# A lower scheduling place for the weight-conversion passes while attention runs alone, in a fused attention and feed-forward kernel

## The chip, the core and the metric

The kernel runs on one core of one Trainium2 chip. The metric is the device time of one execution in microseconds (us). Its five engines work side by side and meet through semaphores: TensorE (PE; its weight loads are shown apart as PEld), VectorE (DVE), ScalarE (ACT), GpSimd (POOL) and SyncE (SP), whose queue issues nearly all DMAs. Each engine executes its own list of instructions strictly in the order in which that list was built.

## What is computed

The reference, cut to what matters:

```python
# 8 batches, 8 heads, 512 local and 32 global positions, head size 64, window 32
out_g = softmax(scale * q_g @ concat(k_g, k_l).T) @ concat(v_g, v_l)
s_ll  = where(|i - j| <= 32, scale * q_l @ k_l.T, -1e9)
out_l = softmax(concat(scale * q_l @ k_g.T, s_ll)) @ concat(v_g, v_l)
x = concat(out_g, out_l), laid out as 4608 tokens x 512
h = x @ w_in                          # 512 x 2048
g = where(h > 0, h, exp(min(h, 0)) - 1)
result = g @ w_out                    # 2048 x 512
```

All inputs are float32, save that the host passes the two weight matrices as 64-bit integers that hold float64 values.

## The kernel before

**Attention** (`attention`, line 643 on) runs over 80 slots, one for each batch, head group of four and tile of 128 positions, and one for the global queries of each group. A slot has four stages, and each is one step of the generator: S (scores, line 769, then the masked negative scores and their minimum on VectorE, L780, and the exponentials on ScalarE, L786), T (transposes of the four probability tiles, L809, copied by L811), U (transposes of the global columns, L742 to L745, copied by L746, L748 and L750) and V (products with the values, L853 and L822, into a bank `h`, copied to `xr` by L859 and reduced by L864 to L868). The normalisation by the row sums is L790, L791 and L795 on VectorE and four L793 on GpSimd. The global slots use L703 and L706, L715 and L716, the exponentials L720 and L722, and L731 and L732 on GpSimd. The probability tiles rotate through three buffers, named p_93, p_94 and p_95 in what follows, and the transposed ones through ptw_81 and ptw_82.

**Feed-forward** (`ffn_stream`) takes blocks of 256 tokens as they get ready. `split_x` (L568, L571) splits a block into two float16 parts `xh` and `xl`; `ffn1` (L324) makes `h` from three products per weight tile; L333 to L349 make the activation and its two parts; `ffn2` (L447, and L482 for blocks that use a seven-product scheme) multiplies with `w_out`.

**Conversion** (`load_weights`, `unit`, lines 157 to 226) turns the weights into two float16 parts. A unit is two of sixteen column groups of `w_in` (m = 0) or row groups of `w_out` (m = 1). Its steps are: s0 (L188 on ScalarE takes the magnitude of the upper words, L189 on GpSimd clamps it), s1a (L193), s1b (L196) and s1c (L200), three VectorE passes over 1024 columns that put the bits together, s1d (L204 on ScalarE, which also sums each partition's bound and thereby gives the raw buffer free), s2 (for w_in, L141 and L142, the maximum over the partitions), s3 (L131 to L136 and L213, the high part) and s4 (L216, the low part). Raw weights come by a DMA on SP's queue (L174) into two buffers in turn. Units 0 to 3 (pairs 0 and 1 of w_in and w_out) and unit 4 (pair 2 of w_in) are started while attention runs alone.

**What sets the order.** The main loop takes one step of attention after the other. While `lead[0]` holds (the first 66 steps) the feed-forward only prepares blocks; after that a table of paces says how many feed-forward steps go with each attention step. `defer(n, fn)` runs a function n ticks later. A scheduler then takes all instructions with a priority that follows the order in which the program wrote them, and builds each engine's list from them: at each point the instruction of the best priority that it holds to be ready. `tc.high_priority(offset=-BEHIND)` with BEHIND = 60 puts what is written inside it 60 places back. Before the change only `add_up` (sums of weight blocks, much later) uses it.

Of the kernel before, what the change touches and what calls it, by code (L numbers as in the profile page):

```python
# [44 lines left out]
BEHIND = 60  # L45
# [15 lines left out]
def attn_ffn(ctx: ExitStack, tc: tile.TileContext, qT, qgT, kT, vT, vgT, vpT, w_in, w_out, mask, out):  # L61
# [28 lines left out]
    def tick():  # L90
        now[0] += 1
        for fn in later.pop(now[0], []):
            fn()

    def drain():
        while later:
            tick()

    lead = [True]

# [76 lines left out]
    def unit(m, p, raw):  # L177
        f = slice(2 * p * P, 2 * (p + 1) * P)
        shape = [P, NC, 2 * P] if m == 0 else [P, 2, DM]
        parts = [w[:, :, f] for w in win] if m == 0 else [w[:, 2 * p:2 * p + 2, :] for w in wout]  # L180
        pw = (pww if m == 0 else pwo)[:, p:p + 1]
        u = ffn.tile(shape, F32, name="cu", bufs=3)
        mx = ffn.tile([P, 4], F32, name="cm", bufs=4)
        high, low = raw[..., 1], raw[..., 0]
        ui = u.bitcast(I32)

        def s0():
            nc.scalar.activation(u, high.bitcast(F32), AF.Abs)  # L188
            nc.gpsimd.tensor_scalar(u, u, FMAX, FMIN, ALU.min, ALU.max)  # L189

        def s1a():
            tc.keep_in_program_order(
                nc.vector.tensor_scalar(ui, ui, 3, 0x3ffffff8, ALU.logical_shift_left, ALU.bitwise_and))  # L193

        def s1b():
            nc.vector.scalar_tensor_tensor(out=ui, in0=high, scalar=-0x40000000, in1=ui,  # L196
                                           op0=ALU.bitwise_and, op1=ALU.bitwise_or)

        def s1c():
            nc.vector.scalar_tensor_tensor(out=ui, in0=low, scalar=29, in1=ui,  # L200
                                           op0=ALU.logical_shift_right, op1=ALU.bitwise_or)

        def s1d():
            nc.scalar.activation(low.bitcast(F32), u, AF.Abs, accum_out=mx[:, m:m + 1])  # L204

        def s2():
            if m == 0:
                all_max(mx[:, 1:2], mx[:, 0:1])

        def s3():  # L210
            power(pw, mx[:, 1:2])
            inverse(mx[:, 3:4], pw)
            nc.scalar.activation(parts[0], u, AF.Copy, scale=mx[:, 3:4])  # L213

        def s4():
            nc.vector.scalar_tensor_tensor(out=parts[1].rearrange("p a b -> p (a b)") if m else parts[1],  # L216
                                           in0=u.rearrange("p a b -> p (a b)") if m else u, scalar=mx[:, 3:4],
                                           in1=parts[0].rearrange("p a b -> p (a b)") if m else parts[0],
                                           op0=ALU.mult, op1=ALU.subtract)

        d = 1 if lead[0] else 2
        lag = 7 if m else 16
        for i, fn in ((1, s0), (1 + d, s1a), (1 + 2 * d, s1b), (1 + 3 * d, s1c), (1 + 4 * d, s1d),
                      (1 + lag, s2), (2 + lag, s3), (3 + lag, s4)):
            defer(i, fn)

    def tables(group):

# [30 lines left out]
    def add_up(p, cross):  # L259


        if not sums:
            sums["rows"] = [ffn.tile([P, NP * 512], F16, name="raw") for _ in range(2)]
            sums["diag"] = [ffn.tile([P, NP * 256], F16, name="cu", bufs=3) for _ in range(2)]
        w = ffn.tile([P, 2, DM], F32, name="cu", bufs=3)
        s = ffn.tile([P, 512], F32, name="tmp", bufs=3)
        d = None if cross else ffn.tile([P, 512], F32, name="tmp", bufs=3)[:, 0:256]
        pr = slice(2 * p, 2 * p + 2)
        flat = [a[:, pr, :].rearrange("p a b -> p (a b)")[:, 256:768] for a in wout]
        rows = [a[:, p * 512:(p + 1) * 512] for a in sums["rows"]]  # L270
        diag = [a[:, p * 256:(p + 1) * 256] for a in sums["diag"]]
        todo = ((flat, s),) if cross else ((rows, s), (diag, d))

        def s0():
            nc.vector.tensor_add(w, wout[0][:, pr, :], wout[1][:, pr, :])

        def s1():
            if cross:
                nc.vector.tensor_sub(s, w[:, 1, :], w[:, 0, :])
            else:  # L280
                nc.vector.tensor_add(s.rearrange("p (a b) -> p a b", a=2), w[:, :, 0:256], w[:, :, 256:512])
                nc.vector.tensor_add(d, w[:, 0, 0:256], w[:, 1, 256:512])

        def s2():
            for dst, src in todo:
                nc.scalar.copy(dst[0], src)

        def s3():
            for dst, src in todo:
                nc.vector.tensor_sub(dst[1], src, dst[0])  # L290
            if cross:
                added.append(p)

        def behind(fn):
            with tc.high_priority(offset=-BEHIND):
                fn()

        for i, fn in enumerate((s0, s1, s2, s3)):
            defer(1 + 2 * i, lambda fn=fn: behind(fn))
# [774 lines left out]
```

## Time and profile before

| | us |
|---|---|
| median of three runs | 953.43 |
| lowest and highest run | 948.69, 953.65 |
| the profiled execution | 954.72 |
| its span from first to last instruction | 952.9 |

The profiled execution lies 1.29 us above the median, and 1.8 us of it lie around the span. In the span PE is busy for 908.5 us, VectorE for 728.1, ScalarE for 670.1 and GpSimd for 271.1. A busy PE is not a PE at its peak, since matmuls are pipelined. The first matmul of the feed-forward starts 77 us into the span. Names in the rows read out<-in; what stands in brackets at a row's end is the time that the engine sat idle before it and what ended that.

### The profile page before, as it was taken

The page shows a single profiled execution, that of the slowest core. Times are in us where ns is not written, and L with a number is a line of the kernel's source. Part 1 is how long each engine was busy: PE and PEld are TensorE (multiplying, and loading weights), DVE is VectorE, ACT ScalarE, POOL GpSimd, SP SyncE. Part 2 cuts the span into 40 slices and gives each one's busy share as a digit, 9 for nine tenths or more (in the row PEclk, how much of TensorE's full clock was granted, in tenths as well). Part 3 has the DMA queues.
Part 4 walks back from the last instruction along what each step waited for, and adds up shares of the span by engine and source line. Part 5 has one row for each costly group of instructions (what it writes and reads, how often), then busy time and mean ns, then how long its engine had stood idle before and what let it go on. Part 6 is the DMA issues. An engine that isn't in the chain of part 4 may idle for free.

```text
span 952.9 us, 23830 instructions
## 1 busy us (share of the span) xinstructions
PE 908.5 (95%) x9216; PEld 727.8 (76%) x9216; DVE 728.1 (76%) x2025; ACT 670.1 (70%) x1584; POOL 271.1 (28%) x483
## 2 busy tenths in 40 slices
PE   6889887899999999999999999999999999999997
PEld 3567564566666788888888888888888888888886
DVE  4988988889967777768776877687777777676566
ACT  5888996776656767757677767677767767666564
POOL 4655481461522322122121212221332312100000
PEclk8779999899999999999999999999999999999999
DMA  6855876331342023101330123102310101000000
GB/s 262 299 179 180 282 224 191 124 123 57 115 157 90 23 100 103 47 26 46 105 121 26 46 78 125 47 27 79 122 49 25 46 23 35 2 23 23 1 24 23
DMA packets 41769, 87.64 MB, mean 92 GB/s; under 512 B 7736, under 2 KB 8888, under 8 KB 41656
## 3 DMA queue, kind: packets, MB, share of 16 engines
q1 hardware_dynamic: 41368, 85.85, 26.6%
q8 instruction: 73, 1.20, 0.5%
q14 instruction: 40, 0.33, 0.1%
q10 hardware_dynamic: 288, 0.26, 0.1%
HBM read 70.89 MB, written 15.20 MB: 90 GB/s over the span
## 4 chain that ended last, share of the span: by engine, by line
PE 67%; DVE 14%; ACT 9%; POOL 3%; issue 3%; DMA 3%; SPq 0%; DVEq 0%; ACTq 0%; POOLq 0%
PE pa L324 25%; PE acc L482 12%; PE h L482 9%; PE acc L447 4%; PE pa L822 3%; PE h L324 3%; PE pa L769 3%; PE pa L809 2%; ACT p L786 2%; DMA raw<-w_out 2%; PE pa L889 2%; DVE gl L345 1%; POOL p L793 1%; DVE cu L196 1%; DVE cu L200 1%
## 5 line engine op out<-in xcount | busy, mean ns | idle before, releaser
L324 PEld LDWEIGHTS <-winh 128*128 128x128 f16 x2160 | 209.4, 98 | 39.2 <-issue 8.4
L793 POOL TENSOR_SCALAR p<-p,sm 128x128 f32<-128x128 f32 x256 | 147.8, 593 | 303.2 <-DVE sm L791 165.0
L324 PE MATMUL pa<-xh,winh 128*128 128x256 f16 x824 | 224.9, 273 | 0.1
L324 PE MATMUL pa<-xl,winh 128*128 128x256 f16 x824 | 224.6, 273 | 0.0
L324 PE MATMUL pa<-xh,winl 128*128 128x256 f16 x824 | 224.6, 273 | 0.0
L361 ACT ACTIVATE gh<-gx,xs 128x896 f16<-128x896 f32 x103 | 107.3, 1042 | 123.1 <-DVE gx L358 123.0
L345 DVE SCALAR_TENSOR_TENSOR gl<-gx,xs,gh 128x896 f16<-128x896 f32 x103 | 119.4, 1159 | 59.9 <-ACT gh L361 59.0
L482 PEld LDWEIGHTS <-gh 128*128 128x128 f16 x1456 | 139.5, 98 | 24.0 <-issue 7.4
L786 ACT ACTIVATE p<-p,m 128x160 f32<-128x160 f32 x256 | 106.7, 421 | 41.6 <-DVE m L780 41.4
L324 PEld LDWEIGHTS <-winl 128*128 128x128 f16 x1080 | 106.1, 98 | 14.3 <-issue 1.2
L333 ACT ACTIVATE g<-pa,xs 128x512 f32<-128x512 f32 x103 | 70.3, 682 | 24.4 <-PE pa L324 23.8
L482 PE MATMUL acc<-wouth,gh 128*128 128x256 f16 x312 | 85.2, 273 | 0.0
L482 PE MATMUL acc<-woutl,gh 128*128 128x256 f16 x312 | 85.1, 273 | 0.0
L335 ACT ACTIVATE g<-g 128x512 f32<-128x512 f32 x135 | 85.0, 630 | 0.1
L482 PE MATMUL acc<-wouth,gl 128*128 128x256 f16 x312 | 85.0, 273 | 0.0
L482 PEld LDWEIGHTS <-gl 128*128 128x128 f16 x728 | 71.2, 98 | 9.2 <-DVE gl L345 1.0
L482 PE MATMUL h<-raw,gh 128*128 128x256 f16 x416 | 75.0, 273 | 0.0
L324 PE MATMUL h<-xh,winh 128*128 128x256 f16 x256 | 71.1, 279 | 1.5 <-ACT hs L334 0.9
L324 PE MATMUL h<-xl,winh 128*128 128x256 f16 x256 | 71.0, 278 | 0.7 <-DVE xl L571 0.7
L324 PE MATMUL h<-xh,winl 128*128 128x256 f16 x256 | 71.0, 278 | 0.0
L780 DVE CUSTOM_DVE_ANT_0 p<-pa,msk 128x160 f32<-128x160 f32 x228 | 61.5, 318 | 4.8 <-PE pa L769 4.7
L342 DVE SCALAR_TENSOR_TENSOR gx<-g,hs 128x512 f32<-128x512 f32 x51 | 35.9, 704 | 36.0 <-ACT g L335 35.6
(236 smaller groups left out, 2016.9 us busy)
## 6 DMA issues: line engine op xcount, KB each, us to landing
k<-kT SPq DMA_DIRECT2D x32, 640.0 KB, 5.1
v<-vT SPq DMA_DIRECT2D x64, 256.0 KB, 2.8
q<-qT SPq DMA_DIRECT2D x32, 256.0 KB, 5.6
raw<-w_in SPq DMA_DIRECT2D x8, 1024.0 KB, 5.9
raw<-w_out SPq DMA_DIRECT2D x8, 1024.0 KB, 6.8
out<-o SPq DMA_DIRECT2D x32, 256.0 KB, 2.3
od<-o SPq DMA_DIRECT2D x24, 256.0 KB, 3.1
o<-od SPq DMA_DIRECT2D x24, 256.0 KB, 2.8
```

Source lines behind the costliest of these rows:

```text
L324: nc.tensor.matmul(h[:, j, :], wt[:, c, f], xt[:, c, :], start=k == 0, stop=k == 11)
L333: nc.scalar.activation(g, hf, AF.Relu, scale=sc[:, p:p + 1])
L335: nc.scalar.activation(g, g, AF.Exp, scale=-1.0)
L342: nc.vector.scalar_tensor_tensor(out=out, in0=ins[0], scalar=-1.0, in1=ins[1], op0=ALU.add, op1=ALU.max)
L345: nc.vector.scalar_tensor_tensor(out=dst, in0=src, scalar=sg, in1=hi, op0=ALU.mult, op1=ALU.subtract)
L361: nc.scalar.activation(gh, gx, AF.Copy, scale=sg)
L447: nc.tensor.matmul(acc[t], gt[:, s], wt[:, f, :], start=p == first and j == 0 and k == 0, stop=p == last and j == 1 and k == 2)
L482: nc.tensor.matmul(cols, gt, w, start=p == 0 and k == 0, stop=last and k == len(todo) - 1, skip_group_check=True)
L769: nc.tensor.matmul(sp[r][half * HQ:(half + 1) * HQ, j * KW:(j + 1) * KW], q[rows, qs], k[rows, t, half, :], start=True, stop=True)
L780: nc.vector.tensor_tensor_reduce(out=p, in0=sp[r][:, j * KW:(j + 1) * KW], in1=msk[:, mi, :], op0=ALU.add, op1=ALU.min, scale=-scale, scal ...
L786: nc.scalar.activation(ps[i], ps[i], AF.Exp, bias=m[:, i:i + 1], scale=-1.0, accum_out=s[:, 0, i:i + 1])
L793: nc.gpsimd.tensor_scalar(ps[i][:, 0:P], ps[i][:, 0:P], s[:, 1, i:i + 1], 1.0, ALU.mult, ALU.mult)
```

## The change

A helper `behind` moves from `add_up` to the head of the kernel, and the deferred steps of a conversion unit are wrapped in it if the unit is started while attention runs alone. Steps s0 and s2 keep their place; s1a to s1d, s3 and s4 get a place 60 back. What is computed stays the same, instruction by instruction.

```diff
+    def behind(fn):
+        with tc.high_priority(offset=-BEHIND):
+            fn()
+
     lead = [True]
...
         lag = 7 if m else 16
         for i, fn in ((1, s0), (1 + d, s1a), (1 + 2 * d, s1b), (1 + 3 * d, s1c), (1 + 4 * d, s1d),
                       (1 + lag, s2), (2 + lag, s3), (3 + lag, s4)):
-            defer(i, fn)
+            defer(i, (lambda fn=fn: behind(fn)) if lead[0] and fn not in (s0, s2) else fn)
...
             if cross:
                 added.append(p)
-
-        def behind(fn):
-            with tc.high_priority(offset=-BEHIND):
-                fn()
 
         for i, fn in enumerate((s0, s1, s2, s3)):
             defer(1 + 2 * i, lambda fn=fn: behind(fn))
```

In the changed kernel the lines of `unit` stand four lower: L188 is L192 there, L193 is L197, L196 is L200, L200 is L204, L204 is L208 and L142 is L146.

The lists of all engines differ in about the first 125 us and are the same, apart from those line numbers, from there to the end. Three places:

VectorE, before, about 43 us into the span, where the three passes of unit 3 stand; the names p_93, p_94 and p_95 are probability tiles of three successive slots:

```order
L795 TENSOR_TENSOR pz<-p_93,sm 128x128
L193 TENSOR_SCALAR cu<-cu 128x1024
L811 COPY ptw_81<-pa 128x2x4x64
L196 SCALAR_TENSOR_TENSOR cu<-raw,cu 128x1024
L142 TENSOR_REDUCE cm<-pa 128x1
L200 SCALAR_TENSOR_TENSOR cu<-raw,cu 128x1024
L753 TENSOR_REDUCE ptg_84<-pa 128x32
L131 TENSOR_SCALAR pww<-cm 128x1
L790 TENSOR_SCALAR sm<-sm 128x4
L780 ISA p_95,m<-pa,msk 128x160
```

VectorE, after, the same passes of unit 3:

```order
L753 TENSOR_REDUCE ptg_84<-pa 128x32
L791 RECIPROCAL sm<-sm 128x4
L780 ISA p_95,m<-pa,msk 128x160
L780 ISA m 128x1
L795 TENSOR_TENSOR pz<-p_94,sm 128x128
L197 TENSOR_SCALAR cu<-cu 128x1024
L811 COPY ptw_82<-pa 128x2x4x64
L200 SCALAR_TENSOR_TENSOR cu<-raw,cu 128x1024
L864 COPY xglob<-h 128x2x32
L868 TENSOR_REDUCE xm<-xr 128x1
L204 SCALAR_TENSOR_TENSOR cu<-raw,cu 128x1024
```

The three passes have moved from behind the slot of p_93 to behind that of p_94, past the four L780 of p_95, and the last of them stands behind the copy L864, which needs a product of PE.

ScalarE, before, about 62 us into the span, around the magnitude pass L188 of unit 5 (the second pair-2 unit, not itself wrapped):

```order
L786 ACTIVATE p_94,sm<-p_94,m 128x160 x2
L188 ACTIVATE cu<-raw 128x1024
L568 ACTIVATE xh<-xr,xm 128x1024
L720 ACTIVATE pg,sg<-pa,mg 128x4x64 x2
L722 ACTIVATE pu,sg<-pa,mg 128x32
L746 COPY ptw_81<-pa 64x4x32
L748 COPY ptw_81<-pa 64x4x32
L750 COPY ptg_84<-pa 128x2x64
L786 ACTIVATE p_95,sm<-p_95,m 128x160
```

ScalarE, after, the same place:

```order
L568 ACTIVATE xh<-xr,xm 128x1024
L786 ACTIVATE p_94,sm<-p_94,m 128x160 x2
L746 COPY ptw_81<-pa 64x4x32
L748 COPY ptw_81<-pa 64x4x32
L750 COPY ptg_84<-pa 128x2x64
L786 ACTIVATE p_95,sm<-p_95,m 128x160
L192 ACTIVATE cu<-raw 128x1024
L720 ACTIVATE pg,sg<-pa,mg 128x4x64 x2
L722 ACTIVATE pu,sg<-pa,mg 128x32
```

The magnitude pass, which waits for a DMA, has moved back by the first L568, three copies and one exponential; the L720 still follow it.

PE, before, at the same time (`wm` and `xm` transposes are L141; ptw_81 and ptw_82 hold transposed tiles of two slots):

```order
L141 MATMUL pa<-ident,xm 128x128
L809 MATMUL pa<-ident,p_94 128x128 x4
L742 MATMUL pa<-ident,pz 128x128
L745 MATMUL pa<-ident,pg 128x128
L769 MATMUL pa<-k,q 64x160 x3
L853 MATMUL h<-ptg_84,ptw_83 64x160 x2
L822 MATMUL h<-ptw_81,v 64x96 x4
L853 MATMUL h<-ptg_84,ptw_83 64x160 x2
L822 MATMUL h<-ptw_81,v 64x96 x4
L769 MATMUL pa<-k,q 64x160 x5
```

PE, after:

```order
L145 MATMUL pa<-ident,xm 128x128
L853 MATMUL h<-ptg_84,ptw_83 64x160 x2
L822 MATMUL h<-ptw_81,v 64x96 x4
L853 MATMUL h<-ptg_84,ptw_83 64x160 x2
L822 MATMUL h<-ptw_81,v 64x96 x4
L809 MATMUL pa<-ident,p_94 128x128 x4
L742 MATMUL pa<-ident,pz 128x128
L745 MATMUL pa<-ident,pg 128x128
L769 MATMUL pa<-k,q 64x160 x8
```

The value products of one slot have moved ahead of the transposes of p_94, and the eight score products stand together behind those.

## Rows read from the trace of the kernel before

**Rows 1.** The page's granted TensorE clock in 40 slices, tenths of 2.4 GHz.

```profile
PEclk8779999899999999999999999999999999999999
```

**Rows 2.** Busy time by stage: length, then PE, PEld, DVE, ACT, POOL, clock, DMA.

```profile
20.00:78.00 58.00, 48.70 (x533) 34.77 (x534) 50.29 (x214) 44.56 (x148) 36.33 (x76) 0.78 0.61 206
78.00:125.00 47.00, 43.62 (x434) 30.66 (x432) 42.10 (x120) 44.73 (x113) 24.24 (x38) 1.00 0.74 253
125.00:260.00 135.00, 120.59 (x951) 79.61 (x949) 121.35 (x269) 99.28 (x207) 59.08 (x77) 0.96 0.41 134
260.00:953.00 693.00, 682.31 (x7199) 576.10 (x7197) 506.65 (x1388) 471.31 (x1083) 142.91 (x271) 1.00 0.17 57
```

**Rows 3.** The same view, of three short stretches of the lead.

```profile
40.00:52.00 12.00, 11.50 (x77) 7.71 (x75) 10.82 (x45) 8.70 (x30) 8.59 (x14) 0.50 0.87 314
...
66.00:68.00 2.00, 0.18 (x1) 0.21 (x2) 1.21 (x1) 2.00 (x8) 1.78 (x4) 0.61 0.04 13
...
70.00:72.00 2.00, 2.00 (x18) 1.48 (x17) 1.56 (x8) 1.49 (x7) 1.72 (x5) 0.50 0.01 4
```

**Rows 4.** Groups by line, first 78 us: busy us, mean ns, idle before.

```profile
L786 ACT ACTIVATE p<-p,m 128x160 f32<-128x160 f32 x49 | 20.5, 423 | 2.5 <-DVE m L780 2.4
...
L200 DVE SCALAR_TENSOR_TENSOR cu<-raw,cu 128x1024 int32<-128x1024 int32 x4 | 5.0, 1239 | 0.0
L196 DVE SCALAR_TENSOR_TENSOR cu<-raw,cu 128x1024 int32<-128x1024 int32 x4 | 4.9, 1217 | 0.0
...
L216 DVE SCALAR_TENSOR_TENSOR winl<-cu,cm,winh 128x1024 f16<-128x1024 f32 x2 | 2.6, 1282 | 0.0
```

**Rows 5.** Timeline of POOL, 41 to 50 us: start, length, instruction, idle before.

```profile
41.02 1.51 POOL L793 TENSOR_SCALAR p<-p,sm 128x128 f32<-128x128 f32 x4 [0.54 <-ACT p L786]
43.51 4.14 POOL L793 TENSOR_SCALAR p<-p,sm 128x128 f32<-128x128 f32 x4 [0.97 <-DVE sm L791]
...
48.86 1.41 POOL L793 TENSOR_SCALAR p<-p,sm 128x128 f32<-128x128 f32 x4
```

**Rows 6.** Timeline of DVE, 44 to 52 us.

```profile
44.86 1.22 DVE L196 SCALAR_TENSOR_TENSOR cu<-raw,cu 128x1024 int32<-128x1024 int32 x1
...
46.20 1.21 DVE L200 SCALAR_TENSOR_TENSOR cu<-raw,cu 128x1024 int32<-128x1024 int32 x1
...
51.90 0.23 DVE L864 COPY xglob<-h 128x64 f32<-128x64 f32 x1 [0.46 <-ACT xr L859]
```

**Rows 7.** Timeline of ACT, 64 to 74 us.

```profile
64.60 1.13 ACT L188 ACTIVATE cu<-raw 128x1024 f32<-128x1024 f32 x1 [1.61 <-DMA raw<-w_out]
65.63 1.13 ACT L568 ACTIVATE xh<-xr,xm 128x1024 f16<-128x1024 f32 x1
66.67 0.46 ACT L720 ACTIVATE pg<-pa,mg 128x256 f32<-128x256 f32 x1
...
73.17 0.37 ACT L859 COPY xr<-h 128x256 f32<-128x256 f32 x1 [1.69 <-PE h L822]
```

**Rows 8.** Timeline of PE, 67 to 78 us.

```profile
67.82 1.08 PE L809 MATMUL pa<-ident,p 128*128 128x128 f32 x4 [2.41 <-ACT pg L720]
...
70.51 0.80 PE L853 MATMUL h<-ptg,ptw 128*64 128x160 f32 x4
...
73.06 0.85 PE L769 MATMUL pa<-k,q 64*64 64x160 f32 x10
...
77.15 0.27 PE L324 MATMUL h<-xh,winh 128*128 128x256 f16 x1
```

**Rows 9.** Timeline of DVE, 66 to 75 us.

```profile
66.79 2.14 DVE L571 SCALAR_TENSOR_TENSOR xl<-xr,xm,xh 128x1024 f16<-128x1024 f32 x1 [1.52 <-ACT xh L568]
...
73.58 0.23 DVE L864 COPY xglob<-h 128x64 f32<-128x64 f32 x1 [1.51 <-ACT xr L859]
...
74.25 0.31 DVE L780 CUSTOM_DVE_ANT_0 p<-pa,msk 128x160 f32<-128x160 f32 x1
```

**Rows 10.** Timeline of SP's queue, 56 to 59 us.

```profile
56.99 0.38 SPq L174 DMA_DIRECT2D raw<-w_out  x1
58.74 0.33 SPq L681 DMA_DIRECT2D v<-vT  x1
```

## The prediction, made before the result was known

> **What bounds the kernel now.** I read the stages first [rows 2]. From 260 us to the end PE is busy 682.31 of 693 us at full clock: nothing that the change touches lies there, and the engines' lists are the same from about 125 us on, so whatever is won or lost before that point is carried to the end as a shift. The stage that the change rearranges is the lead, 20 to 78 us. There no engine is full: VectorE 50.29 of 58 us, PE 48.70, ScalarE 44.56, GpSimd 36.33. So VectorE has 7.7 us of idle time in it, and that is about the most that a better order can take out of the lead. PE's 48.70 are inflated, since the granted clock is 0.78 on average: the page's clock line is below 9 in slices 1, 2, 3 and 4 [rows 1], and the short stretches show why that matters [rows 3]. Between 40 and 52 us and again around 70 us the clock is 0.50, the lower level of 1.2 GHz, and PE is busy nearly all the time; the second of these comes straight after 66 to 68 us, in which PE ran for 0.18 of 2 us. So the lead is a chain that hops between engines, each waiting for another in turn, with PE at half rate after its longest gap. The two waits to look at are the one before that gap, and the one on GpSimd around 44 us.
>
> **The change part by part.** It adds and removes no work. It moves s1a to s1d, s3 and s4 of units 0 to 4 back, past instructions of attention. A pass costs 1.22 to 1.28 us [rows 4], and each that stood before an instruction of attention lets that one go earlier by as much, if nothing else holds it, and is itself due later.
>
> First place, 40 to 57 us. Before, the passes of unit 3 run at 44.86 and 46.20 us [rows 6] while GpSimd normalises p_93, which takes it 4.14 us; the slots on either side take 1.51 and 1.41 [rows 5]. After, they stand behind p_94's slot, and the four L793 of p_93 lie beside the small L780 instead: 4.14 - 1.51 = 2.6 us off that step. The Trainium skill's GPSIMD Engine Reference (Specifications) says that GpSimd's SBUF interface is shared with VectorE and contended by instructions with two SBUF inputs or in a two-port mode; these rows agree. By that rule the loss moves to p_94, beside which the passes now stand. Worked from the rows alone: p_94's step, started at about 46 us and stretched to 4.14, would end at about 50.1 us, against 50.3 before (48.86 + 1.41), so nobody sees it. Of the 2.6 us PE can use only a part, because it is itself busy 11.5 of 12 us at the half clock there [rows 3]; I take 1.2 us at the copy L859 around 51 us. That is given back: before, the last pass and one L216 were done by the time VectorE came to L864, which waited 0.46 us for L859 [rows 6]. After, L204 and both L216 stand behind L864, and VectorE reaches L864 early and waits there for some 2 us with nothing before it. I take half of the 1.2 us as left at 57 us, 0.6, while one L216 of 1.28 us is still due that was done before. The term lies between a gain of 0.6 us (the L216 finds a hole) and a loss of 0.7 (it doesn't: 1.28 - 0.6); I take 0, the middle.
>
> Second place, 62 to 74 us, where most of the sum comes from. Before, ScalarE stands idle for 1.61 us in front of L188, which waits for raw w_out; then come L188 (1.03 us to the next start), L568 (1.04), and only at 66.67 us the L720 that free a bank for PE's L809 of p_94. PE waits 2.41 us for that, to 67.82 us [rows 7, 8]. After, L568, three copies (some 0.27 us each, estimated at two thirds of an exponential's 0.42 [rows 4]) and one exponential go first: 1.04 + 0.8 + 0.42 = 2.26 us, which fills the 1.61. ScalarE was free at 64.60 - 1.61 = 62.99 us, so L720 starts at 62.99 + 2.26 + 1.03 = 66.3 us, 0.4 earlier, and L809 at 67.4. The larger part is on PE. The value products L853 and L822, which before ran from 70.51 to 73.06 us, stand after the change in front of L809. They need the copy L811 on VectorE, which stands behind L571 there: 64.0 + 1.28 for L571, then some 1.0 us to L753, so they start at about 66.4 us. Two bounds follow, by PE's clock. At the half clock they take 2.55 us, to 68.9; L809 to the first three scores take 70.51 - 67.82 = 2.69, to 71.6; the other five scores (73.06 to 73.84, 0.78 us at what was then a rising clock), to 72.4: 1.45 us before 73.84. At the full clock the first two are halved: 66.4 + 1.27 + 1.35 + 0.4 = 69.4, so 4.4 us before. I take the middle, 2.9 us, because the hole on PE is shortened from both sides but not closed. What was late next before was L859 at 73.17 us, 1.69 us idle in front of it for PE's L822, and L864 on VectorE after 1.51 us idle [rows 7, 9]; both come before L780 of the next slot at 74.25 us. With the products ahead these waits go, and the second L571 is next, at about 71 us: 3 us earlier, so it does not cut the term. L324 then starts at about 74.2 instead of 77.15 us [rows 8].
>
> DMAs. Unit 3's s1d gives the raw buffer free for the DMA at 56.99 us [rows 10]; it is moved back behind L864, to about 51.9 + 0.5 + 1.24 + 1.13 = 54.8 us (L864 and the reduction behind it, the pass, and a ScalarE pass as long as L188). That is 2.2 us before SP's queue comes to it, so it costs nothing; if it ends later than 57 us, the queue stops with the value loads of 58.74 us behind it. From 78 to 125 us ScalarE is busy 44.73 of 47 us and VectorE 42.10 [rows 2]; unit 4's passes move by one or two places among them, which I set at nothing, with up to 0.5 us either way, a third of one pass.
>
> The sum: 0 - 2.9 + 0 = -2.9 us against the profiled execution's 954.72 us, which gives 951.8. It lay 1.29 us above the median of the runs; against the median of 953.43 the same sum gives 950.5 us.
>
> **The rivals.** Half a per cent, 4.8 us, is about what a measurement of this kernel can tell from no change.
>
> *Given back.* VectorE and ScalarE have the same work as before, and ScalarE has 2.3 us of idle time between 78 and 125 us. If PE's earlier start at L324 only makes it wait for L333 and L342, the 2.9 us are lost there. For it speaks ScalarE's 44.73 of 47 [rows 2]; against it, that the waits removed at 63 and 73 us are waits of ScalarE and VectorE themselves. Time: 953.4 us.
>
> *The clock stays up.* If PE never goes idle for long, both stretches at 0.50 shrink. The second gives its upper bound of 4.4 us. In the first, PE's 11.5 busy us would be halved, but only the part between p_93's last L793 at 47.65 us and the copy before L864 at 51.90 is on the path, some 4 us, which gives 2. Time: 953.43 - 6.4 = 947.0 us. For it speaks that L853 and L822 now fill the gap; against, that they can start only at 66.4 us.
>
> *SP's queue stops, slower.* The price is above: if unit 3's s1d ends after 57 us, each us later delays the value loads, and with them stage V and PE. PE falls to 1.2 GHz after such a gap, as at 68 us, and 12 us at half rate, as from 40 to 52, cost 6. It decides at 2.2 us more delay than I count. Time: 953.43 + 6 = 959.4 us. For it speaks that L204, L208 and two copies stand in a row behind L864; against, the 2.2 us.
>
> That the change doesn't do what it says is out: the lists show the passes moved.
>
> **How the numbers follow.** The forecast, 950.5 us, 0.47: a gain of 1.45 to 4.4 us with 0.5 either way, 948.5 to 952.5. Given back 0.20, clock up 0.22, queue stops 0.11. The range reaches from 945.5 (1.5 us below the clock case, for the scatter of the three runs) to 956.0 (2.5 above the given-back case, likewise); it leaves out the queue case and the far end of the clock case. Faster by over 0.5% (below 948.7): the clock case and the lowest tenth of the forecast, 0.28. Slower (above 958.2): the queue case, 0.11. Within: 0.61.
>
> **What would show it.** In the profile after: L793 of p_93 near 1.5 us and of p_94 near 4; no DMA wait of over 0.5 us in front of the magnitude pass at 65 us; L853 ahead of L809 with the granted clock above 0.61 in the two us after; L324 first at about 74 us; the end shifted by the same amount. The forecast is wrong if L324 starts at 74 us and the stage to 125 us gives it back, if L324 starts no earlier than 76.5, or if the raw w_out DMA is issued later than 57 us.

## The result

The changed kernel takes 955.72 us (median of 15 runs, 951.78 to 960.72) against 951.29 us for the kernel before (15 runs, 947.94 to 954.94). The ratio is 1.0046 with a 95% interval from 1.0027 to 1.0064: slower by 4.4 us, between 2.6 and 6.1. The forecast was faster by 2.9 us. A second set of runs, after_again below, gave 955.8 us and the same ratio. One run of after_scales_late (5056.73 us), one of scalar_steps_only (1529.8) and one of the kernel before (1528.71) lie far above all others and are left out of every median and ratio here.

The profiled execution of the changed kernel took 955.26 us, 0.5 below its median, and the one of before took 954.72, which is 3.4 above the 951.29 of its fifteen runs. So the two spans, 953.3 and 952.9 us, are nearly equal though the kernels are not: a comparison of the two traces to the end would hide the loss. It has to be read by stages, and from more than one execution. One instruction serves as a mark, on VectorE the L345 behind the fourth L455, just past the place up to which the lists differ. Here it is in before and in the changed kernel:

```profile
132.57 0.75 DVE L345 SCALAR_TENSOR_TENSOR gl<-g,xs,gh 128x512 f16<-128x512 f32 x1 [0.39 <-ACT gh L349]
```

```profile
136.18 0.75 DVE L345 SCALAR_TENSOR_TENSOR gl<-g,xs,gh 128x512 f16<-128x512 f32 x1 [0.39 <-ACT gh L349]
```

The changed kernel is 3.6 us late there. Its second execution comes to the mark at 136.32 us, two more with before's lead (before_again, pair2_only) at 133.93 and 131.95. So the loss is made ahead of 133 us. What follows hides it: from there to 260 us before_again gains 4.1 us on before, though both execute the same lists.

The windows of the changed kernel, by stage, to be set beside [rows 2] (length, then busy us of PE, PEld, DVE, ACT and POOL with counts, granted clock, DMA share, GB/s):

```profile
20.00:78.00 58.00, 42.28 (x523) 31.38 (x524) 50.22 (x215) 45.26 (x153) 38.50 (x77) 0.85 0.60 206
78.00:125.00 47.00, 43.55 (x410) 29.56 (x409) 37.71 (x109) 39.40 (x94) 19.43 (x36) 0.93 0.67 231
125.00:260.00 135.00, 122.33 (x982) 82.01 (x981) 124.29 (x278) 103.00 (x219) 61.16 (x78) 0.97 0.43 141
260.00:953.00 693.00, 682.78 (x7201) 575.96 (x7199) 507.54 (x1390) 471.73 (x1083) 140.14 (x271) 1.00 0.17 57
```

The last stage is as before (682.78 busy us of PE, 682.31 in [rows 2]). In the lead PE's clock is better, 0.85 against 0.78, and PE is busy for 42.28 us instead of 48.70; that much of the hoped-for effect is there, though part of it is chance (a second execution of before has a clock of 0.82). But from 78 to 125 us the clock is 0.93 where it was 1.00, and the row counts 410 instructions of PE there instead of 434 (424 in before_again): the changed kernel enters that stage late.

**First place, 40 to 57 us.** GpSimd, the L793 of p_93 and p_94:

```profile
44.19 1.46 POOL L793 TENSOR_SCALAR p<-p,sm 128x128 f32<-128x128 f32 x4 [2.16 <-DVE cm L146]
46.89 3.06 POOL L793 TENSOR_SCALAR p<-p,sm 128x128 f32<-128x128 f32 x4 [1.24 <-PE pa L809]
```

The L793 of p_93 now take 1.46 us instead of 4.14, and those of p_94 take 3.06 instead of 1.41 [rows 5], as the prediction had it. What it had not is a little later, on ScalarE's timeline and then PE's:

```profile
53.72 0.26 ACT L746 COPY ptw<-pa 64x128 f32<-64x128 f32 x1 [0.48 <-PE pa L745]
53.88 1.13 ACT L208 ACTIVATE raw<-cu 128x1024 f32<-128x1024 f32 x1
55.10 0.26 ACT L748 COPY ptw<-pa 64x128 f32<-64x128 f32 x1
55.39 0.27 ACT L750 COPY ptg<-pa 128x128 f32<-128x128 f32 x1
...
58.77 1.15 ACT L217 ACTIVATE wouth<-cu,cm 128x1024 f16<-128x1024 f32 x1
```

```profile
55.70 0.44 PE L853 MATMUL h<-ptg,ptw 128*64 128x128 f32 x4 [1.65 <-ACT ptg L750]
...
62.34 0.79 PE L769 MATMUL pa<-k,q 64*64 64x160 f32 x16 [1.66 <-ACT ptg L750]
```

Unit 3's s1d (L208) stands between two copies of one slot, L746 and L748. In before the same step ran at 47.44 us, and s3 of `w_out` (L213 there, L217 here, 58.77 us) ran at 53.76, each ahead of where the copies came due. Now PE waits 1.65 and 1.66 us for L750.

**Second place, 62 to 74 us.** ScalarE and then PE, to be set beside [rows 7, 8]:

```profile
67.84 1.11 ACT L192 ACTIVATE cu<-raw 128x1024 f32<-128x1024 f32 x1
68.86 0.45 ACT L720 ACTIVATE pg<-pa,mg 128x256 f32<-128x256 f32 x1
```

```profile
68.94 0.49 PE L853 MATMUL h<-ptg,ptw 128*64 128x160 f32 x4 [0.20 <-DVE ptg L753]
...
70.29 0.65 PE L809 MATMUL pa<-ident,p 128*128 128x128 f32 x4
...
73.42 0.44 PE L853 MATMUL h<-ptg,ptw 128*64 128x128 f32 x4 [1.03 <-ACT ptg L750]
```

The magnitude pass (L192) no longer waits for its DMA, L853 goes ahead of L809, and the granted clock is 1.00 from 66 to 72 us where it was 0.61 and 0.50 [rows 3]. L853 of the next slot starts at 73.42 us; in before it was 73.84:

```profile
73.84 0.44 PE L853 MATMUL h<-ptg,ptw 128*64 128x128 f32 x4
```

So everything that this place gave has only paid for what was lost between 53 and 63 us.

**Third place, 70 to 82 us, which the prediction did not name.** GpSimd, then PE:

```profile
69.57 1.04 POOL L193 TENSOR_SCALAR cu<-cu 128x1024 f32<-128x1024 f32 x1
70.69 0.26 POOL L584 TENSOR_SCALAR xs<-isc,xm 128x1 f32<-128x1 f32 x1
...
71.85 0.26 POOL L588 TENSOR_SCALAR xs<-wm_b,xm 128x1 f32<-128x1 f32 x1
72.08 2.42 POOL L731 TENSOR_SCALAR pk<-pu,sg 32x32 f32<-32x32 f32 x4
74.59 0.69 POOL L732 TENSOR_SCALAR pg<-pg,sg 128x512 f32<-128x512 f32 x1
...
76.05 2.13 POOL L793 TENSOR_SCALAR p<-p,sm 128x128 f32<-128x128 f32 x6
```

```profile
76.48 1.54 PE L809 MATMUL pa<-ident,p 128*128 128x128 f32 x4 [1.31 <-POOL p L793]
...
78.45 0.42 PE L324 MATMUL h<-xh,winh 128*128 128x256 f16 x1
...
82.31 0.77 PE L769 MATMUL pa<-k,q 64*64 64x160 f32 x16
```

In before GpSimd did L731 and L732, and only then the small scales of the second block, L584 to L588:

```profile
69.69 1.36 POOL L731 TENSOR_SCALAR pk<-pu,sg 32x32 f32<-32x32 f32 x4 [1.83 <-ACT ptw L746]
...
71.81 0.27 POOL L584 TENSOR_SCALAR xs<-isc,xm 128x1 f32<-128x1 f32 x1
...
74.01 2.59 POOL L793 TENSOR_SCALAR p<-p,sm 128x128 f32<-128x128 f32 x4
```

Here six of the scales go first, most likely because both chains became ready at once (the last VectorE steps before them, L728 and L140, start at 70.53 and 70.61 us; in before they, L728 and L136, were at 69.38 and 71.00). L731 starts at 72.08, beside the VectorE pass L571 (72.03 us, 1.32), and takes 2.42 us. The L793 of p_95 start at 76.05 us instead of 74.01. PE waits 1.31 us for them, its clock falls (0.74 from 75 to 80 us), and the first of the L324 run at half rate (0.42 us each instead of 0.27): the first 24 last from 78.45 to 82.31 us, 3.86 us where before took 2.71 (77.15 to the L769 at 79.86).

### The profile page after: what moved, and what is told of

It reads as the page before. It is cut to its first block, busy times and chain, and to the rows that moved or that the text cites. A ratio compares the mean times of both kernels' runs of the same rounds, so it can differ in the third digit from the quotient of the medians.

```text
span 953.3 us, 23839 instructions
## 1 busy us (share of the span) xinstructions
PE 904.5 (95%) x9216; PEld 725.6 (76%) x9216; DVE 727.3 (76%) x2025; ACT 669.6 (70%) x1584; POOL 267.8 (28%) x483
## 4 chain that ended last, share of the span: by engine, by line
PE 68%; DVE 15%; ACT 9%; issue 3%; POOL 2%; DMA 2%; SPq 0%; DVEq 0%; ACTq 0%; POOLq 0%
PE pa L324 25%; PE acc L482 12%; PE h L482 9%; PE acc L447 4%; PE h L324 4%; PE pa L822 4%; PE pa L769 3%; PE pa L809 2%; ACT p L786 2%; PE pa L889 2%; DVE gl L345 1%; DVE cu L200 1%; DVE cu L204 1%; DVE g L342 1%; PE pa L703 1%
## 5 line engine op out<-in xcount | busy, mean ns | idle before, releaser
L324 PEld LDWEIGHTS <-winh 128*128 128x128 f16 x2160 | 209.4, 98 | 39.8 <-issue 8.8
L793 POOL TENSOR_SCALAR p<-p,sm 128x128 f32<-128x128 f32 x256 | 141.1, 567 | 310.2 <-DVE sm L791 169.5
L324 PE MATMUL pa<-xh,winh 128*128 128x256 f16 x824 | 224.9, 273 | 0.1
L324 PE MATMUL pa<-xl,winh 128*128 128x256 f16 x824 | 224.6, 273 | 0.0
L324 PE MATMUL pa<-xh,winl 128*128 128x256 f16 x824 | 224.6, 273 | 0.0
L345 DVE SCALAR_TENSOR_TENSOR gl<-gx,xs,gh 128x896 f16<-128x896 f32 x103 | 119.6, 1161 | 59.9 <-ACT gh L361 59.0
L324 PEld LDWEIGHTS <-winl 128*128 128x128 f16 x1080 | 106.1, 98 | 14.2 <-issue 1.0
L324 PE MATMUL h<-xh,winh 128*128 128x256 f16 x256 | 71.2, 280 | 2.0 <-ACT hs L334 1.4
L324 PE MATMUL h<-xl,winh 128*128 128x256 f16 x256 | 71.1, 279 | 0.7 <-DVE xl L571 0.7
L324 PE MATMUL h<-xh,winl 128*128 128x256 f16 x256 | 71.0, 278 | 0.0
L780 DVE CUSTOM_DVE_ANT_0 p<-pa,msk 128x160 f32<-128x160 f32 x228 | 61.3, 318 | 8.0 <-PE pa L769 7.9
```

The costliest lines, as they stand in the source:

```text
L324: nc.tensor.matmul(h[:, j, :], wt[:, c, f], xt[:, c, :], start=k == 0, stop=k == 11)
L345: nc.vector.scalar_tensor_tensor(out=dst, in0=src, scalar=sg, in1=hi, op0=ALU.mult, op1=ALU.subtract)
L780: nc.vector.tensor_tensor_reduce(out=p, in0=sp[r][:, j * KW:(j + 1) * KW], in1=msk[:, mi, :], op0=ALU.add, op1=ALU.min, scale=-scale, scal ...
L793: nc.gpsimd.tensor_scalar(ps[i][:, 0:P], ps[i][:, 0:P], s[:, 1, i:i + 1], 1.0, ALU.mult, ALU.mult)
```

## Experiments

Theories after the result. **A**: the loss is made at 53 to 63 us by the late ScalarE steps. **B**: it is made after 80 us by unit 4. **C**: it is made at 70 to 82 us by GpSimd's order and PE's clock behind it. **D**: chance arrivals of raw weights decide, not the order. All ratios are to the kernel before.

### One pair alone

The two kernels differ from the changed one in one line:

```diff
-            defer(i, (lambda fn=fn: behind(fn)) if lead[0] and fn not in (s0, s2) else fn)
+            defer(i, (lambda fn=fn: behind(fn)) if lead[0] and p == 1 and fn not in (s0, s2) else fn)
```

and `p == 2` for the other.

> Only units 2 and 3 (pair 1) have their steps put back; pairs 0 and 2 stay as before the change. Theory A (units 2 and 3 lose about 3.0 us at 53 to 63 us, because their late ScalarE steps s1d and s3 run ahead of attention's copies, win 3.4 at 63 to 74 and lose 2.4 at 74 to 82, where GpSimd is late and the clock falls): about 1 to 2.5 us above the kernel before, ratio 1.001 to 1.0026, and the first L324 at 77 to 79 us. Theory B (the loss is made after 90 us, by unit 4): the same as before within 1 us, ratio 0.999 to 1.001. Theory D (only chance waits for raw weights differ): ratio 1.000, and no steady shift behind 82 us.

> Only unit 4 (pair 2 of w_in) has its steps put back; everything up to about 80 us is as before the change. Theory A: ratio 0.999 to 1.001, since unit 4's passes were set at nothing within 0.5 us. Theory B: the whole 4.4 us, ratio 1.0046, with the shift made between 85 and 130 us.

Measured: pair 1 alone 954.32 us, ratio 1.003 (1.001 to 1.0051); pair 2 alone 950.52 us, ratio 1.0004 (0.9982 to 1.0027). B's full loss (1.0046) lies outside the interval of pair 2 alone, and its L345 mark lies at 131.95 us against 135.00 with pair 1 alone: units 2 and 3 carry most of the loss, so B is not the main cause. PE in pair1_only:

```profile
71.75 0.44 PE L853 MATMUL h<-ptg,ptw 128*64 128x128 f32 x4 [1.04 <-ACT ptg L750]
...
74.79 1.02 PE L809 MATMUL pa<-ident,p 128*128 128x128 f32 x3 [1.30 <-POOL p L793]
76.38 0.48 PE L809 MATMUL pa<-ident,p 128*128 128x128 f32 x1 [0.57 <-POOL p L793]
...
77.29 0.42 PE L324 MATMUL h<-xh,winh 128*128 128x256 f16 x1
...
81.07 0.77 PE L769 MATMUL pa<-k,q 64*64 64x160 f32 x16
```

L853 comes at 71.75 us, 2.1 us earlier than in before. Then the L809 wait for GpSimd's L793 twice, 1.30 and 0.57 us, and the first 24 L324 take 3.78 us. This kernel is ahead at 72 us and behind at 81: not what A says, and what C says.

In pair2_only the lists are those of before up to about 77 us, so it is also another execution of that lead. ScalarE there:

```profile
62.54 1.14 ACT L192 ACTIVATE cu<-raw 128x1024 f32<-128x1024 f32 x1
```

No wait for raw `w_out`, where [rows 7] has 1.61 us. The largest wait that the forecast wanted to fill is not there in every execution.

### ScalarE's steps alone, VectorE's passes alone

```diff
-            ... if lead[0] and fn not in (s0, s2) else fn)
+            ... if lead[0] and fn in (s1d, s3) else fn)
```

and `(s1a, s1b, s1c, s4)` for the other.

> Only the ScalarE steps (s1d, and s3 with its small VectorE operations) are put back; the VectorE passes s1a, s1b, s1c and s4 keep the place of before. Theory A in its narrow form (ScalarE's s1d and s3 come late because VectorE's passes in front of them come late): with the passes in place nothing is lost at 53 to 63 us, ratio 0.998 to 1.001. Rival (the place of the ScalarE steps itself is what costs): 3 to 4.4 us, ratio 1.003 to 1.0046.

> Only the VectorE passes (s1a, s1b, s1c, s4) are put back; s1d and s3 keep the place of before. Theory A in its narrow form: the ScalarE steps wait for the late passes all the same and then run ahead of the copies with full preference, so the loss at 53 to 63 us stays: 3 to 5 us above before, ratio 1.003 to 1.005. Rival (the place of the ScalarE steps itself is what costs): ratio 0.997 to 1.001.

Measured: ScalarE's steps alone 955.12 us, ratio 1.0032 (1.0012 to 1.0052); VectorE's passes alone 953.02 us, ratio 1.0016 (0.9997 to 1.0035). The narrow form of A falls: with the passes in place the ScalarE steps cost as much, and the passes alone cost less than was expected. By their numbers the rival fares better: 1.0032 lies in its range (1.003 to 1.0046), 1.0016 just above its other one (0.997 to 1.001), with an interval that reaches into both theories' ranges. But the traces show another wait than the rival names. In both PE waits for GpSimd again, for the L793 of p_94 in scalar_steps_only, which stand behind the eight scales of the first block there (first row of PE's timeline below; ScalarE had also waited 2.00 us for raw `w_out` at 63.36 us), and for those of p_95 in vector_passes_only (second):

```profile
69.49 1.52 PE L809 MATMUL pa<-ident,p 128*128 128x128 f32 x4 [2.69 <-POOL p L793]
```

```profile
72.60 1.42 PE L809 MATMUL pa<-ident,p 128*128 128x128 f32 x4 [1.61 <-POOL p L793]
...
74.45 0.42 PE L324 MATMUL h<-xh,winh 128*128 128x256 f16 x1
...
78.52 0.78 PE L769 MATMUL pa<-k,q 64*64 64x160 f32 x16
```

VectorE's passes alone bring the first L324 to 74.45 us, 2.7 us before the kernel before, but the 24 matmuls take 4.07 us, the first 13 of them at about half rate, so that half of it is lost by 78.5 us.

### Before once more

> The kernel before, profiled a second time. Theory D (the 1.61 us that ScalarE waited for raw w_out at 64.60 us, and the 3.09 us at 158.9 us, are chance arrivals of two DMAs in one execution): in this profile at least one of the two waits is below 0.5 us, the first L324 comes at 75.9 to 77.2 us, and the time is 949 to 951 us where the wait at 159 us is missing and 953 to 955 us where it is there. Rival (both waits belong to the kernel): 1.6 and 3 us again, first L324 at 77.1 us.

Measured: 952.15 us, one run. ScalarE waited 1.90 us for raw `w_out`:

```profile
64.08 1.12 ACT L188 ACTIVATE cu<-raw 128x1024 f32<-128x1024 f32 x1 [1.90 <-DMA raw<-w_out]
```

and 1.01 us at 157.64 us, where the first execution waited 3.09; the first L324 came at 77.01 us. The expectation asked for one wait below 0.5 us, so as written it was missed. With pair2_only there are three executions of this lead: the wait was 1.61, 1.90 and 0 us, the first L324 came at 77.15, 77.01 and 75.92. A fourth execution with the same lists up to 70 us (before_scales_late) waited 1.48 us, so three of four had a wait of 1.5 to 1.9. D is right in that a microsecond in the lead, and up to three at 159 us, are chance; it does not explain a ratio that two sets of runs gave alike.

### GpSimd's scales behind the L793

The eight scales of the second block are queued on GpSimd behind the four L793 of p_95. No other engine's list changes. This is not the order of before, where all eight stand ahead of these L793.

```diff
-                        return group, blk, xh, xl, scales(group, mx), seven
+                        return group, blk, xh, xl, late(scales, group, mx), seven
...
-                    nc.gpsimd.tensor_scalar(ps[i][:, 0:P], ps[i][:, 0:P], s[:, 1, i:i + 1], 1.0, ALU.mult, ALU.mult)
+                    norms.append(nc.gpsimd.tensor_scalar(ps[i][:, 0:P], ps[i][:, 0:P], s[:, 1, i:i + 1], 1.0, ALU.mult, ALU.mult))
...
+    def late(fn, *a):
+        calls.append(1)
+        if len(calls) not in (3, 4):
+            return fn(*a)
+        with tc.issue_after(norms[43].ins):
+            return fn(*a)
```

> The changed kernel, with the eight small GpSimd operations of the second block's scales (L584 to L588, 2.2 us together) held behind the four L793 of p_95; the lists of the other engines stay as they are. Theory C (the late L793 of p_95 and the fall of the clock behind it cost 2.4 us at 74 to 82 us): L793 of p_95 starts at 73 to 74 us instead of 76.05, the first L324 comes at 75.5 to 77 us instead of 78.45, and the time falls by 2 to 3.5 us against the changed kernel's 955.7, ratio to before 1.001 to 1.0025. Rival (PE and VectorE set that place, GpSimd's lateness is covered): no change, ratio 1.0046.

Measured: 952.22 us, ratio 1.0026 (1.0003 to 1.0049). That is 3.5 us below the changed kernel's median and 1.9 us by the ratios, whose intervals overlap. GpSimd's timeline, PE's, and the window from 75 to 80 us:

```profile
70.46 1.36 POOL L731 TENSOR_SCALAR pk<-pu,sg 32x32 f32<-32x32 f32 x4 [0.79 <-DVE xm L140]
71.91 1.56 POOL L732 TENSOR_SCALAR pg<-pg,sg 128x512 f32<-128x512 f32 x1
73.90 1.18 POOL L793 TENSOR_SCALAR p<-p,sm 128x128 f32<-128x128 f32 x3 [0.43 <-DVE sm L791]
```

```profile
73.02 0.44 PE L853 MATMUL h<-ptg,ptw 128*64 128x128 f32 x4 [1.91 <-ACT ptg L750]
...
74.69 1.12 PE L809 MATMUL pa<-ident,p 128*128 128x128 f32 x4
...
75.97 0.27 PE L324 MATMUL h<-xh,winh 128*128 128x256 f16 x1
...
78.69 0.77 PE L769 MATMUL pa<-k,q 64*64 64x160 f32 x16
```

```profile
75.00:80.00 5.00, 4.97 (x53) 3.91 (x52) 4.87 (x21) 4.36 (x19) 4.66 (x12) 1.00 0.16 52
```

The L853 starts at 73.02 us, within 0.1 us of after_again's 73.05. From there on there is no wait for L793, the clock is 1.00 from 75 to 80 us, the first L324 comes at 75.97, and the 24 take 2.72 us. At this place C is shown: it was worth 2 us before the L324 and 1.1 in them. The gain is still there at the L345 mark, 132.04 us against 136.18 and 136.32, which is level with the kernel before (132.57 and 133.93).

### s1d held behind the copies

Unit 3's s1d is queued on ScalarE behind the L750 of the slot whose copies it split (`copies` collects the L750, number 6 is that one). No other engine's list changes.

```diff
-            nc.scalar.activation(low.bitcast(F32), u, AF.Abs, accum_out=mx[:, m:m + 1])
+            hold(nc.scalar.activation(low.bitcast(F32), u, AF.Abs, accum_out=mx[:, m:m + 1]), 6 if (m, p) == (1, 1) else None)
```

> The changed kernel, with one ScalarE instruction moved by two places: s1d of unit 3 (L208 at 53.88 us) is held behind the copies L748 and L750 that it ran ahead of; the lists of the other engines stay as they are. Theory A (PE's 1.65 us wait for L750 at 55.70 us is a loss on the path): PE's L853 starts at 54.5 to 54.8 instead of 55.70 us and everything behind it comes about 1 us earlier, 954.4 to 955.0 us, ratio to before 1.0033 to 1.004. Rival (the wait only takes the place of another one at 56 to 63 us): no change within 0.3 us, ratio 1.0046.

Measured: 954.29 us, ratio 1.0044 (1.0029 to 1.006). PE:

```profile
54.55 0.44 PE L853 MATMUL h<-ptg,ptw 128*64 128x128 f32 x4 [0.54 <-ACT ptg L750]
...
56.47 0.55 PE L822 MATMUL h<-ptw,v 128*64 128x96 f32 x8 [0.47 <-DVE pwo L136]
...
58.29 0.32 PE L145 MATMUL pa<-ident,wm_b 128*128 128x128 f32 x1 [0.73 <-DVE sg L727]
...
61.97 0.79 PE L769 MATMUL pa<-k,q 64*64 64x160 f32 x16 [1.66 <-ACT ptg L750]
```

L853 starts at 54.55 us, 1.15 earlier, as expected. It buys nothing: PE now waits 0.47 and 0.73 us for VectorE behind it, and the L769 of 61.97 us still waits 1.66 for L750, 0.37 us earlier than in the changed kernel and no earlier than in after_again (61.94). The rival holds: taking away this one wait only uncovers the next, since s3 and four exponentials still stand ahead of the second group of copies.

### VectorE's passes of pairs 0 and 1, with the scales held

```diff
-            ... if lead[0] and fn not in (s0, s2) else fn)
+            ... if lead[0] and p < 2 and fn in (s1a, s1b, s1c, s4) else fn)
```

together with the hold of the scales.

> Only the VectorE passes (s1a, s1b, s1c, s4) of pairs 0 and 1 are put back, and the second block's scales on GpSimd are held behind the L793 of p_95. If theories A and C are right, this keeps the earlier start of the value products and leaves out the late ScalarE steps, the late L793 and pair 2: first L324 at 73 to 75 us, 948.5 to 950.5 us, ratio to before 0.997 to 0.9995. Rival (the lead has other limits, and what is won up to 80 us is given back by 125 us): ratio 1.000 to 1.002.

Measured: 950.19 us, ratio 1.0005 (0.9984 to 1.0026). The first L324 came at 75.94 us, later than the 73 to 75 expected: in this execution PE's clock was 0.81 from 65 to 70 us and 0.85 from 70 to 75, where vector_passes_only had 1.00 in the first of these. It was also the slowest of the twelve runs (956.82 us). Not faster than before; the rival's ratio stands for this one.

### The changed kernel again, and two more holds

> The changed kernel, timed and profiled a second time beside the two kernels below. Theory C: L793 of p_95 starts at 75 to 77 us again, PE waits about 1 us for it, the granted clock falls at 76 to 82 us and the first 24 L324 take 3.5 to 4 us instead of 2.5; ratio to before 1.003 to 1.0055. Rival (the late L793 was chance in one execution): the first 24 L324 in 2.5 us, started before 77.5 us.

Measured: 955.8 us, ratio 1.0046 (1.0027 to 1.0064). The L793 of p_95 at 75.66 us, 1.30 us of wait on PE, the first L324 at 78.07 and the 24 in 3.88 us. The third place is no chance of one execution.

> The change for pairs 0 and 1 alone (VectorE and ScalarE steps of units 0 to 3), unit 4 as before, and the second block's scales on GpSimd held behind the L793 of p_95. If GpSimd's lateness is all that the change costs in the lead and unit 4 costs nothing: first L324 at 75.5 to 77 us, 949.5 to 952.5 us, ratio 0.999 to 1.002. Rival (what is left of the loss, 1 to 2.5 us, is made before 70 us by the late passes of pair 1): ratio 1.002 to 1.0035.

The edit is `p < 2` in the line of `defer`, with the hold. Measured: 951.06 us, ratio 0.9996 (0.9978 to 1.0013): nothing is left of the loss. Against after_scales_late only unit 4 differs. That would be 2.8 us for unit 4, but the two intervals overlap, and pair2_only, with unit 4 alone, lost nothing. At the L345 mark this kernel is at 133.10 us, no earlier than after_scales_late's 132.04, so the traces show no such cost up to there. What unit 4's passes cost in company of the others stays open.

> The kernel before, with the second block's scales on GpSimd held behind the L793 of p_95; its lists change in other places too, since the planner answers to the hold. In before GpSimd is hardly late there (PE waits 0.15 us for L793 in the execution without the wait for raw w_out), so theory C expects little: first L324 0 to 0.7 us earlier, ratio 0.9985 to 1.0005. If GpSimd's 2.2 us of scales were on the path in before too: ratio 0.997 to 0.9985, and this kernel would be the fastest of all.

Measured: 949.09 us, ratio 0.999 (0.9965 to 1.0015). In the trace only GpSimd's list differs from before's, at 71 to 76 us; the expectation that other places change too did not come true. The first L324 came at 74.55 us, 2.6 before the kernel before and more than the 0.7 expected. It was given back at once:

```profile
78.00:125.00 47.00, 44.25 (x398) 30.67 (x395) 40.29 (x116) 40.52 (x101) 19.80 (x36) 0.89 0.73 244
```

The row counts 398 instructions of PE between 78 and 125 us, where before has 434 [rows 2], and the clock was 0.89 instead of 1.00; the L345 mark is at 133.13 us, 0.6 behind before. An earlier start of the feed-forward is not yet an earlier end.

> The run of pair 1 alone (ratio 1.003, first L324 at 77.29 us after waits of 1.30 and 0.57 us for L793), now with the second block's scales held behind the L793 of p_95. Theory C: neither wait for L793, first L324 about 3 us behind the L853 before it as in the other two kernels with the hold, so at 74.5 to 75.5 us, and 2 to 3.5 us less than pair 1 alone: ratio 0.9985 to 1.001. If the gain in the lead reached the end in full, it would be the fastest kernel, ratio 0.997 to 0.998. Rival (in pair 1's kernel the loss is made elsewhere): ratio 1.002 to 1.004.

Measured: 949.68 us, ratio 0.9993 (0.9971 to 1.0014), from 1.003 without the hold. The first L324 came at 76.27 us, not at 74.5 to 75.5, since PE waited 2.06 us for L750 ahead of its L853; the part behind it is as expected, 2.96 us. The L345 mark moves from 135.00 us without the hold to 131.65.

All the lead's executions in one table; L853 and the first L324 are starts on PE's timeline, L853 being the first one of the slot ahead of the L809 of p_95, "24 L324" is the time from the first L324 to the L769 behind the first 24, and L345 is the start of the mark on VectorE:

| kernel | L853 | first L324 | between | 24 L324 | L345 | ratio |
|---|---|---|---|---|---|---|
| before | 73.84 | 77.15 | 3.31 | 2.71 | 132.57 | |
| before_again | 73.53 | 77.01 | 3.48 | 2.71 | 133.93 | |
| pair2_only (same lead) | 72.29 | 75.92 | 3.63 | 2.71 | 131.95 | 1.0004 |
| the changed kernel | 73.42 | 78.45 | 5.03 | 3.86 | 136.18 | 1.0046 |
| after_again | 73.05 | 78.07 | 5.02 | 3.88 | 136.32 | 1.0046 |
| after_s1d_held | 73.06 | 77.83 | 4.77 | 4.21 | 136.22 | 1.0044 |
| pair1_only | 71.75 | 77.29 | 5.54 | 3.78 | 135.00 | 1.003 |
| scalar_steps_only | 74.52 | 77.85 | 3.33 | 2.71 | 134.78 | 1.0032 |
| vector_passes_only | 68.99 | 74.45 | 5.46 | 4.07 | 133.23 | 1.0016 |
| after_scales_late | 73.02 | 75.97 | 2.95 | 2.72 | 132.04 | 1.0026 |
| no_pair2_scales_late | 73.77 | 76.72 | 2.95 | 2.71 | 133.10 | 0.9996 |
| pair1_scales_late | 73.31 | 76.27 | 2.96 | 2.72 | 131.65 | 0.9993 |
| before_scales_late | 71.78 | 74.55 | 2.77 | 2.72 | 133.13 | 0.999 |
| vector_passes_scales_late | 73.18 | 75.94 | 2.76 | 2.72 | 134.70 | 1.0005 |

The columns "between" and "24 L324" sum to 6.0 to 6.3 us with the order of before, 8.9 to 9.3 with GpSimd's new order, and 5.5 to 5.7 with the hold. The first two differ by 2.7 us or a little more. At the mark the three executions of the changed kernel's order that keep the scales in their place lie 3.6 to 3.8 us behind before and 2.2 to 2.4 behind before_again, and the hold takes 4.1 to 4.3 us back there, 3.4 with pair 1 alone. That is all of the loss as far as single executions can tell. Why after_scales_late, level with before at the mark, still has a ratio of 1.0026 was not settled; the mark is of one execution, the ratio of many.

Two rows don't fit the one order. vector_passes_only keeps GpSimd's order of before and has 9.5 us all the same: PE comes to its L853 4.9 us earlier and runs into the eight scales that stand ahead of the L793. scalar_steps_only loses nothing in these columns; its wait for the L793 of p_94 comes before them. In both, scales on GpSimd stand ahead of the L793 that PE waits for, as in the changed kernel.

## Why the prediction was wrong

The step that failed, as the runs show, is the one behind the -2.9: "the second L571 is next", so that L324 starts at about 74.2 us. L324 started at 78.45 us. What came next was GpSimd, whose L793 PE waited 1.31 us for, and behind that wait the lower clock; neither has a term in the sum. A second step, the 0 of the first place, was 3.0 us off in this execution; its cause is in part argued. Both are taken up below, in the order of the sum.

- **First place, term 0.** The GpSimd steps came out as said (1.46 and 3.06 us), and so, nearly, did the gain at L859 (50.54 against 51.49 us, 0.95 for 1.2). What failed is the sentence that sets the balance at 57 us between +0.6 and -0.7 by that gain and one L216: it counted VectorE's work and left out what follows on ScalarE, s1d and s3 falling due in front of attention's copies. At the first L780 of the slot of p_94 the changed kernel is 3.0 us late (63.30 against 60.30 us). Three more executions with the same lists up to there (in one of them with s1d held) had 62.91, 62.93 and 63.63, and before had 59.69 and 60.14 in two more, so this is no chance of one execution. A fifth had 60.91 (after_scales_late): there the clock was 1.00 from 40 to 50 us, in the other four 0.66 to 0.70. The two kernels that move pair 1 alone, also at 1.00 there, had 60.96 and 61.05, with PE still waiting 1.54 and 1.55 us for L750. So some 2 of the 3 us went with the clock. What the late ScalarE steps cost by themselves is argued and not shown; the one wait that was taken away gave nothing back.
- **Second place, -2.9.** The mechanism held, and the size against this execution of before. From that 3.0 us behind, the changed kernel was 0.4 ahead at L853 (73.42 against 73.84), a gain of 3.4. The wait for raw `w_out` was gone, L853 ran ahead of L809, the clock was 1.00. But the step took the 1.61 us from one execution; another of the same lists had none of it, and reached its L853 at 72.29 us. Against that one the gain is 2.0 (3.2 behind at the first L780, 1.1 at L853).
- **"What is late next."** Here the sum broke. The prediction asked the question of L859 and L864 and answered with the second L571. GpSimd was not looked at beyond the L793 of p_93 and p_94, though what ends PE's wait for L809 is GpSimd's L793. Filling ScalarE's gap put L720 behind other work, so L731 became ready later (L720 at 68.86 us against 66.67), while the second block's scales became ready at the same moment; the list puts six of the scales first. That cost 2 us at L809 and, by the clock, 1.1 more. With the scales held, both are gone.
- **DMAs, nothing.** This failed in form: the raw `w_out` DMA went out at 58.92 us, not 56.99, behind a value load. Unit 3's s1d ended at 55.0 us, close to the estimated 54.8, so it was not what held the DMA back. The prediction named a DMA later than 57 us as a sign that it was wrong. The rival that went with it did not happen, since L192 stood further back and waited for nothing.
- **78 to 125 us, nothing either way.** Not shown right or wrong. Unit 4 alone cost nothing measurable; with the other pairs the ratios leave room for some 2.8 us, of which the mark at 133 us shows nothing.
- **Base of the sum, and the shift.** The prediction put the profiled execution 1.29 us above the median of three runs; against fifteen it lies 3.4 above. Its wait of 3.09 us for raw `w_out` at 159 us (last section) is one reason. It does not change the sign, but it makes the forecast time itself 2.1 us too high before any term is added. Nor is what is lost before 125 us simply carried to the end: between 133 and 260 us two executions of before shift by 4.1 us against each other, as much as the loss itself. In [rows 1] the slices below 9 are 1, 2, 3 and 8, not 4; no term rests on that.
- **The rivals.** The slower rival had the right sign and the second half of its mechanism (a gap on PE, then half the clock), with the wrong engine as the cause. The gap came from GpSimd and not from SP's queue, at 76 us and not at 60. "Given back" was seen in before_scales_late, where 2.6 us won in the lead were gone by the end.

The Trainium skill's GPSIMD Engine Reference (Specifications), which the prediction used for the first place, says that GpSimd shares its SBUF interfaces with VectorE. The runs agree at the third place too: the four L731 took 2.42 us beside L571 and 1.36 us apart from it, and when the hold moved L731 ahead, L732 fell beside L571 and took 1.56 us instead of 0.69.

## What to carry to other kernels

When a change lets an instruction go earlier, follow it on every engine down to the next point at which PE waits, and ask there which engine's list decides; the small instructions of an engine that is not full were what the scheduler moved here without being asked. Where a sum rests on one wait for a DMA, look at a second execution before counting it. And an order that costs PE one gap of 1.3 us can cost nearly as much again when the clock falls behind it, as it did here (1.1 us).

## What the runs showed of the hardware

One raw `w_out` DMA of 1024 KB, issued at 56.99, 55.91 and 56.38 us in three executions of the same order, was waited for until 64.60 and 64.08 us and had landed before 62.54 in the third: 7.6, 8.2 and at most 6.2 us from issue. In before_scales_late, with the same lists up to 70 us, it was issued at 55.78 and waited for until 63.50 us, 7.7 us. At 159 us the wait of the same kind of pass was 3.09, 1.01 and 0.20 us in the first three executions; the first and the last of these, on ScalarE's timeline of before and of pair2_only:

```profile
158.91 1.12 ACT L188 ACTIVATE cu<-raw 128x1024 f32<-128x1024 f32 x1 [3.09 <-DMA raw<-w_out]
```

```profile
155.54 1.17 ACT L192 ACTIVATE cu<-raw 128x1024 f32<-128x1024 f32 x1 [0.20 <-DMA raw<-w_out]
```

The three executions with these waits took 954.72, 952.15 and 950.15 us (the third is pair2_only, whose lists differ from before's between about 77 and 125 us).

With the same lists up to there, PE's clock fell in different places: from 40 to 50 us it was 0.66 in the changed kernel and 1.00 in after_scales_late, which then had 0.50 from 60 to 65 us. After a gap of 1.3 us that ended 1.7 to 2.5 us before the first L324 it fell in all four executions with GpSimd's new order (the 24 L324 took 3.78 to 4.21 us); after a gap of 1.9 or 2.1 us that ended 3.0 us before the first L324 it was not low at the L324 (2.72 us).
